# Local and pooled attention ahead of two feed-forward layers: the first stage put into the list schedule, with 1 KB loads by head pair and local products on GpSimd

## The chip, the cores and the metric

The kernel runs on one core of a Trainium2 chip. The metric is the device time in microseconds of one execution; smaller is better. Engines: PE (TensorE; PEld its weight loads), DVE (VectorE), ACT (ScalarE), POOL (GpSimd) and SP (SyncE, which issues most DMAs).

## The reference

Queries, keys and values are float32 arrays of 4 x 8 x 576 x 64 (batch, heads, rows, head size).

```python
q_d = q.reshape(B, H, Sd, factor, D).mean(axis=3)     # factor 4; k_d, v_d likewise
out_d = sm_attn(q_d, k_d, v_d)                        # softmax attention over 144 pooled rows
out_up = np.repeat(out_d, factor, axis=2)
mask = np.abs(pos[:, None] - pos[None, :]) < factor   # local attention: 7 neighbours
scores = np.where(mask, scale * np.matmul(q, k.transpose(0, 1, 3, 2)), -1000000000.0)
out_local = np.matmul(softmax(scores), v)
x = out_up + out_local                                # 2304 tokens x 512
h = x @ w_in;  x = (h - np.tanh(h)) @ w_out           # 512 -> 2048 -> 512
h = x @ w_in2; y = (h * np.cos(h)) @ w_out2           # 512 -> 2048 -> 512
```

## The kernel before

The 2304 tokens are cut into chunks: the first 512 rows of each batch make chunks 0 to 3 (128 partitions by four rows; chunk 1 is worked on as two halves of 256), and the last 64 rows of all four batches (the left-over rows) make chunk 4. Each feed-forward matrix is split into a high and a low float32r part, so each product is three matmuls of 128x128 weights against 512 (or 256) columns.

**The first stage** (`first_attention`, lines 452 to 692) computes the attention of chunk 0 with PE. Per head pair `u` (NP = 4) there are pooled steps: `P.s` (scores, maximum), `P.e` (three exponentials with sums), `P.n` (product on POOL, L398), `P.t` and `P.t2` (transposes), `P.v` (product with the summed values). Per block `i` of 64 rows (NB = 8) there are local steps: `b_s` (mask and scores into a bank of three), `b_m` (maximum, subtraction, exponential in the bank), `b_n` (sum, reciprocal, product into SBUF, all on DVE, L618 to L621), `b_t` (transpose). Per pair of blocks, `b_v` multiplies with v, adds the pooled part (L642) and copies to `xh`; `b_l` subtracts to `xl`. The inputs come by `load_nat` (128 rows of all heads, 256 KB, runs of 256 B, L496), are transposed by `tr` (four transposes) and summed by fours in `red_k` (DVE) and `red_q` (POOL); left-over rows come by `load_lo` and go through `tr_l`. `vsum` sums v by fours on POOL (L303, L304).

The order of these steps is written by hand: each has a time (`keyed`, L656 ff.), the steps are sorted by it and emitted, and each PE step is followed by one matmul `idle<-zero` (`warm`, L479), which computes nothing. Three weight tiles are prepared (`W1.tick`) and chunk 1's first loads issued (`early`, L1118) at times of the same list. In one engine, instructions run in the order in which they were emitted.

**The planner** (`Plan`, L33) orders the rest of attention and the first feed-forward layer. A step has an engine, a duration, a due time `t`, the steps it comes after and the buffers it takes. `run` picks, for each engine, among the steps that could start within `SLACK` of the earliest the one with the smallest due time, and emits the earliest of these. Due times come from constants: `LENGTHS` and `SPANS` for chunks, `LOADEARLY`, `WEARLY` and `WLOAD` for loads and weights. Attention of the later chunks uses POOL for products of 128x896 (`prod_s` L709, `prod_v` L758) and DVE for their sums. The first layer's groups (`group`, L981) write `h` tiles of two buffers; the first two groups run in halves of 256 columns, the four halves in the order a, a, b, b. The weights take ACT (L218, L220, L237), DVE (L228) and POOL (L244) each. The second layer follows, in the order of the program.

## Time and profile before

| what | us |
|---|---|
| median of 3 runs | 902.53 (901.45 to 902.73) |
| the profiled execution | 904.6 |
| its span | 902.7 |
| PE, PEld busy | 886.4, 747.0 |
| DVE, ACT, POOL busy | 571.4, 486.2, 406.2 |

The page gives busy time by engine, the span in 40 slices, the DMA queues, the chain of work that ended last, and the costliest groups of instructions. In the rows below, `x` with a number counts instructions; "[2.24 <-DVE gl L1000]" is idle time ahead of an instruction and what ended it. The granted clock is a share of 2.4 GHz. Matmuls overlap, so the busy time of PE counts time that is shared.

### The profile page before, as it was taken

The page shows a single profiled execution, that of the slowest core. Times are in us where ns is not written, and L with a number is a line of the kernel's source. Part 1 is how long each engine was busy: PE and PEld are TensorE (multiplying, and loading weights), DVE is VectorE, ACT ScalarE, POOL GpSimd, SP SyncE. Part 2 cuts the span into 40 slices and gives each one's busy share as a digit, 9 for nine tenths or more (in the row PEclk, how much of TensorE's full clock was granted, in tenths as well). Part 3 has the DMA queues.
Part 4 walks back from the last instruction along what each step waited for, and adds up shares of the span by engine and source line. Part 5 has one row for each costly group of instructions (what it writes and reads, how often), then busy time and mean ns, then how long its engine had stood idle before and what let it go on. Part 6 is the DMA issues. An engine that isn't in the chain of part 4 may idle for free.

```text
span 902.7 us, 13649 instructions
## 1 busy us (share of the span) xinstructions
PE 886.4 (98%) x4954; PEld 747.0 (83%) x4954; DVE 571.4 (63%) x958; ACT 486.2 (54%) x1024; POOL 406.2 (45%) x447
## 2 busy tenths in 40 slices
PE   9989998999999999999999999999999999999997
PEld 5677785999998888888899888888888888888896
DVE  5789878889999863852245577454536453655453
ACT  4768887335444433373269876454535453544464
POOL 7489999998988971730026343011101110111110
PEclk9999999999999999999999999999999999999999
DMA  9687746423332231461037431010001100100100
GB/s 211 198 281 236 238 132 191 146 86 114 93 104 80 64 85 31 143 186 34 1 120 232 126 108 47 1 47 16 32 1 46 47 1 6 42 23 1 47 2 24
DMA packets 65957, 81.73 MB, mean 91 GB/s; under 512 B 21984, under 2 KB 46566, under 8 KB 65890
## 3 DMA queue, kind: packets, MB, share of 16 engines
q1 hardware_dynamic: 64562, 76.01, 27.8%
q0 software_dynamic: 1232, 4.72, 1.7%
q8 instruction: 39, 0.64, 0.3%
...
## 4 chain that ended last, share of the span: by engine, by line
PE 88%; POOL 4%; ACT 3%; DVE 2%; SPq 1%; DMA 1%; issue 1%; POOLq 0%; ACTq 0%; DVEq 0%
PE h L951 42%; PE oacc L1213 22%; PE acc L977 20%; POOL pr L709 1%; PE pa_s L377 1%; PE pa_t L408 1%; SPq L496 1%; POOL o L244 1%; POOL pr L758 1%; PE pa_x L796 1%; DMA lpt<-in_v_dram 1%; ACT pe L390 1%; PE pa_v L436 1%; PE pa_v L439 0%; DMA raw<-in_moe_w_in_dram 0%
## 5 line engine op out<-in xcount | busy, mean ns | idle before, releaser
L1213 PE MATMUL oacc<-o,i 128*128 128x512 f32 x864 | 209.0, 391 | 0.0
L951 PE MATMUL h<-xh,i 128*128 128x256 f32 (+1 forms) x784 | 203.6, 338 | 2.8 <-DVE gl L1000 2.2
L977 PE MATMUL acc<-gh,o 128*128 128x512 f32 (+1 forms) x768 | 203.2, 342 | 0.9 <-POOL o L244 0.8
L1228 POOL TENSOR_SCALAR y<-y 128x512 f32<-128x512 f32 (+1 forms) x80 | 46.3, 579 | 327.4 <-ACT y L1226 312.2
L951 PE MATMUL h<-x2h,i 128*128 128x512 f32 (+1 forms) x640 | 192.9, 369 | 0.0
L1213 PEld LDWEIGHTS oacc<-o,i 128*128 128x128 f32 x864 | 161.1, 188 | 34.6 <-ACT i L964 0.4
L951 PEld LDWEIGHTS h<-xh,i 128*128 128x128 f32 x784 | 135.8, 191 | 18.5 <-issue 2.9
L977 PEld LDWEIGHTS acc<-gh,o 128*128 128x128 f32 x768 | 134.0, 191 | 17.9 <-POOL o L244 2.9
L951 PEld LDWEIGHTS h<-x2h,i 128*128 128x128 f32 x640 | 116.7, 188 | 21.7
L709 POOL TENSOR_TENSOR pr<-qt,kt 128x896 f32<-128x896 f32 x56 | 119.1, 2137 | 31.0 <-DVE o L762 24.6
L951 PE MATMUL h<-xl,i 128*128 128x256 f32 (+1 forms) x392 | 131.3, 335 | 0.3 <-DVE xl L649 0.3
L977 PE MATMUL acc<-gl,o 128*128 128x512 f32 (+1 forms) x384 | 129.5, 338 | 0.3 <-DVE gl L1000 0.2
L951 PE MATMUL h<-x2l,i 128*128 128x512 f32 (+1 forms) x320 | 117.9, 369 | 0.0
L758 POOL TENSOR_TENSOR pr<-vt,s 128x896 f32<-128x896 f32 x56 | 107.5, 1939 | 1.6 <-DVE o L762 0.3
L1233 DVE TENSOR_TENSOR h<-h,rr 128x512 f32<-128x512 f32 (+1 forms) x80 | 51.6, 645 | 81.8 <-ACT rr L1232 81.6
L1231 ACT ACTIVATE rr<-rr 128x512 f32<-128x512 f32 (+1 forms) x80 | 47.1, 589 | 100.4 <-DVE rr L1230 100.2
L951 PEld LDWEIGHTS h<-xl,i 128*128 128x128 f32 x392 | 74.8, 191 | 7.5 <-DVE xl L649 0.6
L968 ACT ACTIVATE gh<-h 128x512 fp32r<-128x512 f32 x72 | 42.9, 596 | 70.3 <-PE acc L977 62.5
L977 PEld LDWEIGHTS acc<-gl,o 128*128 128x128 f32 x384 | 73.4, 191 | 8.4 <-DVE gl L1000 1.1
L1235 DVE TENSOR_TENSOR i<-h,i 128x512 fp32r<-128x512 f32 (+1 forms) x80 | 50.7, 634 | 45.5 <-ACT i L964 45.4
L994 ACT ACTIVATE th<-h 128x512 f32<-128x512 f32 x64 | 38.2, 597 | 72.5 <-PE h L951 72.4
L1226 ACT ACTIVATE y<-h 128x512 f32<-128x512 f32 (+1 forms) x80 | 44.2, 553 | 59.9 <-PE h L951 59.7
(183 smaller groups left out, 1243.2 us busy)
## 6 DMA issues: line engine op xcount, KB each, us to landing
...
kt<-in_k_dram SPq DMA_DIRECT2D x16, 256.0 KB, 3.7
vt<-in_v_dram SPq DMA_DIRECT2D x16, 256.0 KB, 4.2
...
out_dram<-os SPq DMA_DIRECT2D x16, 256.0 KB, 2.1
```

The source lines that it names most:

```text
L709: nc.gpsimd.tensor_tensor(out=pr.rearrange("p j f d -> p j (f d)"), in0=view(L["q", h], [[0, OFF], [1, 2 * D]], off=f * D), in1=view(L["k" ...
L758: nc.gpsimd.tensor_tensor(out=pr.rearrange("p f d j -> p j f d"), in0=view(L["v", h], [[D, OFF], [D, 2], [1, D]], off=f * D), in1=view(L[" ...
L951: nc.tensor.matmul(hp[:, cs], lhsT=wt[:, kk * 128:(kk + 1) * 128], rhs=xt, start=(kk + c == 0), stop=(kk == KD - 1 and c == 2))
L968: nc.scalar.activation(gh, hp, AF.Copy)
L977: nc.tensor.matmul(acc[e], lhsT=wt[:, e * 128:(e + 1) * 128], rhs=gt, start=(f == 0 and i == 0), stop=(f == KF - 1 and i == 2))
L994: nc.scalar.activation(th, hp, AF.Tanh)
L1213: nc.tensor.matmul(acc[t], lhsT=gt[:, t * 128:(t + 1) * 128], rhs=wt, start=(g == 0 and a_ == 0), stop=(g == KF - 1 and a_ == 2))
L1226: iy = nc.scalar.activation(y, hp, AF.Copy, scale=INV_TWO_PI, bias=ROUND)
L1228: ip = nc.gpsimd.tensor_scalar(out=y, in0=y, scalar1=-ROUND, scalar2=-TWO_PI_HI, op0=ALU.add, op1=ALU.mult)
L1231: nc.scalar.activation(r, r, AF.Abs)
L1233: nc.vector.tensor_tensor(out=hp, in0=hp, in1=r, op=ALU.mult)
L1235: nc.vector.tensor_tensor(out=G[f][1], in0=hp, in1=G[f][0].bitcast(F32), op=ALU.subtract)
```

## The change

- `load_nat` fetches the 512 rows of one head pair, four rows (1 KB) to a partition and head. `tr` makes eight matmuls with the identity of it, 64 output partitions each, and the copies put the rows back in order.
- `red_q` writes its sum straight into `qz`; the factor 1/16 moves into the scores' maximum (a small DVE operation) and the exponential's scale. `pooled_q` on ACT goes; `left_q` becomes a step per head pair.
- `b_m` writes its exponentials to SBUF (`ce`, four buffers); `b_n` sums from there, and POOL makes the product (`NORMB` is all "P").
- `lpt` is zeroed by DVE and not by POOL.
- All steps of the first stage are steps of the one planner, with due times by the longest chain behind them (`tails`). The planner runs until the stage's last `xl` is placed, then the pools are exchanged, and it runs on. The filler matmuls (448 columns) follow the plan's gaps on PE in the first run, and no longer each step.
- The first five weight tiles and chunk 1's loads and products are steps too, open to the planner from the start. The first layer's due times begin at `TB` = 44. Buffers and constants of the later stages stay.

The diff, cut to its core:

```diff
+    def tails(self, steps, end):
+
+        tail = {}
+        for o in reversed(steps):
+            d = o.size / 350e3 + 2.1 if o.size else o.dur
+            o.tail = max(d + LATENCY, o.tail_min) + tail.get(o, 0.0)
+            o.t = end - o.tail
+            for a in o.after:
+                tail[a] = max(tail.get(a, 0.0), o.tail)
+            if o.prev is not None:
+                tail[o.prev] = max(tail.get(o.prev, 0.0), o.tail - o.prev.dur)
...
+            if fill and o.eng == "PE":
+                fill(int((r - self.free["PE"] - 0.1) / 0.2))
...
+            if self.ps_t:
+                nc.vector.tensor_scalar(out=m, in0=m, scalar1=1.0 / (R * R), scalar2=None, op0=ALU.mult)
...
-                nc.scalar.activation(e_[:, i, :], a[:, i, :], AF.Exp, bias=m[:, i:i + 1], accum_out=rs[:, i:i + 1])
+                nc.scalar.activation(e_[:, i, :], a[:, i, :], AF.Exp, bias=m[:, i:i + 1], scale=1.0 / (R * R) if self.ps_t else 1.0, accum_out=rs[:, i:i + 1])
...
-                nc.tensor.matmul(idle, lhsT=zero[:, 0:128], rhs=zero)
+                nc.tensor.matmul(idle[:, 0:448], lhsT=zero[:, 0:128], rhs=zero[:, 0:448])
...
-        def load_nat(nm, t):
-            G[nm, t] = g = lp.tile([128, H, D], F32, tag="g", name=nm + "g", bufs=12)
-            nc.sync.dma_start(out=g, in_=rows_of(q if nm == "q" else k, 0, 128 * t, 128))
+        def load_nat(nm, u):
+            G[nm, u] = g = lp.tile([128, 2, R, D], F32, tag="g", name=nm + "g", bufs=12)
+            nc.sync.dma_start(out=g.rearrange("p e f d -> p e (f d)"),
+                              in_=(q if nm == "q" else k)[0, 2 * u:2 * u + 2, 0:512, :].rearrange("h (p f) d -> p h (f d)", f=R))
...
+            G["vl"] = xp.tile([128, H, R, D], F32, tag="xl", name="lpt")
+            nc.vector.memset(G["vl"], 0.0)
...
-        def tr(nm, t):
-            g = pairs(G.pop((nm, t)))
-            a = ps_a.tile([128, NP, 128], F32, tag="a", name="pa_tr")
-            for u in range(NP):
-                nc.tensor.transpose(a[:, u, :], g[u], ident)
+        def tr(nm, u):
+            g = G.pop((nm, u))
+            a = ps_a.tile([128, R, 128], F32, tag="a", name="pa_tr")
+            for f in range(R):
+                for e in range(2):
+                    nc.tensor.matmul(a[64 * e:64 * e + 64, f, :], lhsT=g[:, e, f, :], rhs=ident)
+            yield
             if nm == "q":
-                nc.scalar.activation(qT[:, :, 128 * t:128 * t + 128], a, AF.Copy, scale=0.125)
+                nc.scalar.activation(qT[:, u, :].rearrange("p (g f) -> p f g", f=R), a, AF.Copy, scale=0.125)
+            elif KEVAC[u] == "A":
+                nc.scalar.activation(kT[:, u, R - 1:R - 1 + 512].rearrange("p (g f) -> p f g", f=R), a, AF.Copy)
             else:
-                nc.vector.tensor_copy(kT[:, :, R - 1 + 128 * t:R - 1 + 128 * t + 128], a)
+                nc.vector.tensor_copy(kT[:, u, R - 1:R - 1 + 512].rearrange("p (g f) -> p f g", f=R), a)
...
+        def red_q(u):
+            half = lp.tile([128, 128, 2], F32, tag="qh", name="qh", bufs=2)
+            q4 = qT[:, u, :].rearrange("p (g f) -> p g f", f=R)
+            nc.gpsimd.tensor_tensor(out=half, in0=q4[:, :, 0:2], in1=q4[:, :, 2:4], op=ALU.add)
+            for e in range(2):
+                p0 = 64 * e
+                nc.gpsimd.tensor_tensor(out=qz[p0:p0 + 64, u, QW * e:QW * e + 128], in0=half[p0:p0 + 64, :, 0], in1=half[p0:p0 + 64, :, 1], op=ALU.add)
+
+        def left_q(u):
+            for e in range(2):
+                nc.gpsimd.tensor_scalar(out=view(qz, [[2, LG], [1, 2]], off=u * 3 * 128 + QW * e + 128, p0=64 * e, n=64),
+                                        in0=view(klq, [[1, LG], [0, 2]], off=NP * 64 + u * 64, p0=64 * e, n=64),
+                                        scalar1=float(R * R), scalar2=None, op0=ALU.mult)
...
-        def pooled_q():
-            for e in range(2):
-                nc.scalar.activation(qz[64 * e:64 * e + 64, :, QW * e:QW * e + 128], qd[64 * e:64 * e + 64], AF.Copy, scale=1.0 / (R * R))
-            for u in range(NP):
-                P.left_q(u)
...
-            exps.append(nc.scalar.activation(s, s, AF.Exp).ins)
+            yield
+            G["e", i] = lp.tile([128, NP, NK], F32, tag="ce", name="ce", bufs=4)
+            nc.scalar.activation(G["e", i], s, AF.Exp)
...
+            rs = sums[:, i]
...
-            nc.vector.tensor_tensor(out=et, in0=s, in1=view(r, [[1, NP], [0, NK]]), op=ALU.mult)
+            yield
+            eng = nc.gpsimd if NORMB[i] == "P" else nc.vector
+            eng.tensor_tensor(out=et, in0=et, in1=view(r, [[1, NP], [0, NK]]), op=ALU.mult)
...
-        with_pe = (tr, tr_l, b_s, b_t, b_v)
-        keyed = [(-9.08, masks), (-2.95, load_vl), (-1.21, load_vg), (13.94, pooled_k), (14.57, pooled_q), (23.6, load_w)]
...
+        add, run = plan.add, plan.chain
+        n0 = len(plan.steps)
+        marks = []
+        small, large = 1.9, 1.1
+        ld, xt, xl, red, vs, up_, sc, bt = {}, {}, {}, {}, {}, {}, {}, {}
+        for t in range(NT_):
+            for nm in "kq":
+                ld[nm, t] = add("SP", 0.47, 0.0, lambda nm=nm, t=t: load_nat(nm, t), new=[("g", f"{nm}g{t}")], size=128 * 2048 * large)
+        for j in range(2):
+            for nm in "kq":
+                ld[nm, "l", j] = add("SP", 0.94, 0.0, lambda nm=nm, j=j: load_lo(nm, j), new=[("k" if j else "g", f"{nm}l{j}")], size=128 * 2048 * small)
+        ld["vg"] = add("SP", 0.47, 0.0, load_vg, size=128 * 8192 * large)
+        ld["vl"] = add("SP", 1.9, 0.0, load_vl, size=64 * 8192 * large)
+        for i in range(NB):
+            ld["vw", i] = add("SP", 0.47 if i else 1.41, 0.0, lambda i=i: load_vw(i), new=[("g", f"vw{i}")], size=NK * 2048 * small)
+        for t in range(NT_):
+            for nm in "kq":
+                a = f"tr{nm}{t}"
+                xt[nm, t] = run(tr(nm, t), 0.0, [
+                    ("PE", 0.92, dict(new=[("ps_a", a)], use=[f"{nm}g{t}"])), ("DVE", 0.72, dict(use=[a])) if nm == "k" and KEVAC[t] == "D" else ("ACT", 0.63, dict(use=[a]))],
+                    after=[ld[nm, t]])[-1]
+                marks += [(o, EARLY[t]) for o in (ld[nm, t], xt[nm, t].prev, xt[nm, t])]
+        late = []
+        for j in range(2):
+            for nm in "kq":
+                a = f"trl{nm}{j}"
+                k0 = len(plan.steps)
+                xl[nm, j] = run(tr_l(nm, j), 0.0, [
+                    ("PE", 0.87, dict(new=[("ps_a", a)], use=[f"{nm}l{j}"])), ("DVE", 0.32 if j else 0.5, dict(use=[a])) if nm == "k" else ("ACT", 0.3, dict(use=[a]))],
+                    after=[ld[nm, "l", j]])[-1]
+                late += [ld[nm, "l", j]] * j + plan.steps[k0:] * j
+        for t in range(NT_):
+            red["k", t] = add("DVE", 0.64, 0.0, lambda t=t: red_k(t), after=[xt["k", t]])
+            red["q", t] = add("POOL", 1.45, 0.0, lambda t=t: red_q(t), after=[xt["q", t]], new=[("qh", f"qh{t}")])
+            red["l", t] = add("POOL", 0.45, 0.0, lambda t=t: left_q(t), after=[xl["q", 0]])
+            marks += [(red[x, t], EARLY[t]) for x in "kql"]
+        pk = add("POOL", 0.24, 0.0, pooled_k, after=[xl["k", 0]])
+
+        for nm, o_ in (("vg", vd), ("vl", vl)):
+            for u in range(NP):
+                vs[nm, u] = add("POOL", 1.2, 0.0, lambda o_=o_, nm=nm, u=u: vsum(o_, nm, u), after=[ld[nm]])
...
+        for i in range(NB):
+            c = f"cs{i}"
+            k0 = len(plan.steps)
+            o = add("PE", 0.9, 0.0, lambda i=i: b_s(i), new=[("ps_1", c)],
+                    after=list(xt.values()) + [xl["k", 0]] * (i == NB - 1))
+            o = run(b_m(i), 0.0, [("DVE", 0.92, dict(use=[c], new=[("cm", f"cm{i}")])), ("ACT", 0.4, dict(use=[c], new=[("ce", f"ce{i}")]))], after=[o])
+            o = run(b_n(i), 0.0, [("DVE", 0.88, dict(use=[f"ce{i}"], new=[("cr", f"cr{i}")])),
+                                  ("POOL", 0.8, dict(use=[f"cr{i}"])) if NORMB[i] == "P" else ("DVE", 0.46, dict(use=[f"cr{i}"]))], after=o)[-1]
+            bt[i] = run(b_t(i), 0.0, [("PE", 0.47, dict(new=[("ps_a", f"cpt{i}")], use=[f"ce{i}"])), ("ACT", 0.62, dict(use=[f"cpt{i}"]))], after=[o])[-1]
+            marks += [(x, BLOCK[i]) for x in plan.steps[k0:]]
+        out = []
+        for j in range(NB // 2):
+            a = f"po{j}"
+            o = run(b_v(j), 0.0, [
+                ("PE", 1.1, dict(new=[("ps_1", a)], use=[f"vw{i}" for i in (2 * j, 2 * j + 1)], after=[bt[2 * j], bt[2 * j + 1], ld["vw", 2 * j], ld["vw", 2 * j + 1]])),
+                ("PE", 0.95, dict(use=[a], after=list(up_.values()))) if UADD[j] == "P" else ("DVE", 0.72, dict(use=[a], after=list(up_.values()))), ("ACT", 0.62, dict(use=[a], new=[("x", "x0")] if j == 0 else [], after=list(vs.values())))],
+                prev=o[0] if j else None)
+            o.append(add("DVE", 0.7, 0.0, lambda j=j: b_l(j), after=o[-1:], use=[a]))
+            out.append(o[-1])
+            o[0].tail_min = 1.2
+        plan.tails(plan.steps[n0:], FEND)
+        marks += [(o, VSUM) for o in vs.values()] + [(o, LOADFIRST) for o in plan.steps[n0:] if o.eng == "SP"] + [(o, OUTS) for o in out]
+        for o, d in marks:
+            o.t += d
+        for o in late:
+            o.t = LATEL - o.tail
+        return out, warm
...
-    TL = 26.5
-    HALVES, XLAST, RAWLAST = 2, 1.68, 3.91
+    TB, FEND, LATEL = 44.0, 20.0, 60.0
+    NORMB = "PPPPPPPP"
+    KEVAC = "DDDD"
+    UADD = "DDDD"
+    LOADFIRST, VSUM, OUTS = 0.00, 0.00, 0.00
+    EARLY = 0.00, 0.50, 1.00, 1.50
+    POOLED = -3.00, -2.50, -2.00, -1.50
+    BLOCK = 0.00, 0.20, 0.40, 0.60, 0.80, 1.00, 1.20, 1.40
+    NF, WFIRST, WLOADF = 5, 3.0, 16.0
+    HALVES = 2
...
+                o = plan.add("PE", mm, t, lambda j=j: second(j), after=[done[j]] + [gate] * (ci == 0) + [wready.get(("o", f)) for f in fs],
...
+            if k < NF:
+                t, slot = need(kind, f) - WFIRST, "raw"
+            ld[k] = plan.add("SP", 0.4, t - (WLOAD if k >= NF else WLOADF), lambda: W1.load(raw_a), after=[gate] if k == NF else [], prev=ld.get(k - 1), new=[(slot, names[k])], size=128 * 4096)
+            bg[k] = plan.chain(W1.begin_parts(), t - 9.0, [
+                ("ACT", 0.65, dict(new=[("wf", wf)] + [("ps_a", wp)] * (k >= NF), use=[names[k]], after=[ld[k]])), ("ACT", 0.67, dict(use=[names[k]]))])
+            md[k] = plan.chain(W1.mid_parts(), t - 7.0, [
+                ("DVE", 0.7, dict(use=[names[k], wf] + [wp] * (k >= NF))),
+                ("POOL" if k < 3 else "ACT", 0.63, dict(use=[wf], new=own))], after=bg[k])
...
-    add_events(first_attention(chunks[0]), 0.0)
-    loaded = {}
-
-    def early(h, which):
-        loaded[h, which] = load_qkv(chunks1[1], h, which, True)
-
-    events += [(TL + 0.02 * i, 0, lambda h=h, x=x: early(h, x)) for i, (h, x) in enumerate([(h, x) for h in range(3) for x in "qk"] + [(h, "v") for h in range(2)])]
-    events += [(TE + TD * i, 0, lambda: W1.tick(raw_a, nc.gpsimd)) for i in range(KE)]
-    events.sort(key=lambda x: x[0])
     sched = tc.manual_schedule()
     sched.__enter__()
-    run_events(1e9)
+    plan = Plan(dict(q=3, k=3, v=3, pr=2, s=3, m=2, r=2, o=8, qkd=2, vd=3, kT=1, pe=1, pt=1, pm=2, pr_=2, up=7, ps_a=2, ps_h=2, acc=4,
+                     th=2, gh=2, gl=2, x=1, raw=2, wf=3, i15=1, o15=1, i14=1, o14=1,
+                     g=12, qh=2, ps_1=3, cm=3, cr=3, ce=4), {}, dict(PE=5.0, ACT=6.4, DVE=2.5, POOL=7.3, SP=0.0))
+    first, warm_ = first_attention(plan, chunks[0])
+    gate = Step(None, 0.0, 0.0, None, (), None, (), 0)
...
+    plan.run(AHEAD, first, warm_)
+    gate.start = gate.end = max(o.start for o in first)
...
```

## Rows read from the trace of the kernel before

**Rows 1.** Stage windows: length; busy by engine (instructions); granted clock; DMA share; GB/s

```profile
5.00:25.00 20.00, 19.37 (x183) 14.15 (x182) 14.30 (x35) 8.95 (x24) 14.36 (x32) 1.00 1.07 225
30.00:35.00 5.00, 4.59 (x55) 2.76 (x57) 3.96 (x15) 3.38 (x13) 3.31 (x6) 1.00 1.07 368
...
7.77:50.87 43.10, 41.15 (x480) 30.25 (x479) 32.55 (x83) 26.44 (x75) 24.75 (x44) 1.00 0.79 201
...
57.30:62.00 4.70, 4.69 (x14) 3.71 (x15) 4.26 (x6) 2.63 (x8) 4.70 (x5) 0.64 0.97 316
130.00:162.00 32.00, 28.07 (x132) 20.63 (x131) 25.99 (x51) 23.68 (x63) 30.91 (x33) 0.95 0.58 177
162.00:503.00 341.00, 340.66 (x2148) 304.59 (x2147) 229.64 (x361) 161.13 (x371) 210.41 (x181) 1.00 0.34 103
```

(In the windows the engines stand in the order PE, PEld, DVE, ACT, POOL.)

**Rows 2.** Timeline at the first layer's start: start, length, engine, line, instruction, idle

```profile
48.14 0.20 PEld L951 LDWEIGHTS h<-xh,i 128*128 128x128 f32 x1
...
57.31 0.47 PE L951 MATMUL h<-xh,i 128*128 128x512 f32 x1 [2.24 <-DVE gl L1000]
```

**Rows 3.** Groups by line, DVE, 0 to 51: busy us, mean ns | idle before

```profile
L618 DVE TENSOR_REDUCE cs<-cs 128x4 f32<-128x280 f32 x8 | 3.6, 454 | 1.7 <-ACT cs L611 1.7
L621 DVE TENSOR_TENSOR ce<-cs,cr 128x280 f32<-128x280 f32 x8 | 3.6, 449 | 0.3
...
L649 DVE TENSOR_TENSOR xl<-pa_o,xh 128x512 fp32r<-128x512 f32 x4 | 2.7, 687 | 0.8 <-ACT xh L645 0.7
...
L392 DVE TENSOR_SCALAR pa_s<-pa_s 128x3 f32<-128x3 f32 x4 | 0.7, 166 | 2.0 <-ACT pe L390 1.9
```

**Rows 4.** Groups by line, POOL, 0 to 51.4

```profile
L244 POOL TENSOR_TENSOR i<-wf,i 128x512 fp32r<-128x512 f32 x3 | 3.9, 1300 | 0.0
L303 POOL TENSOR_TENSOR vg<-vg 128x256 f32<-128x256 f32 x4 | 2.9, 728 | 0.0
...
L582 POOL TENSOR_TENSOR qh<-qT 128x256 f32<-128x256 f32 x4 | 2.5, 613 | 3.4 <-ACT qT L558 3.3
L235 POOL CAST i<-wf 128x512 fp32r<-128x512 f32 x3 | 1.8, 613 | 9.9 <-DVE wf L228 9.9
L304 POOL TENSOR_TENSOR vl<-lpt 128x128 f32<-128x128 f32 x4 | 1.8, 456 | 0.3
...
L295 POOL MEMSET lpt<- 128x2048 f32 x1 | 1.8, 1814 | 0.0
L369 POOL COPY qz<-klq 64x32 f32<-64x32 f32 x8 | 1.7, 206 | 0.4
L583 POOL TENSOR_TENSOR qd<-qh 128x128 f32<-128x128 f32 x4 | 1.6, 400 | 0.3
...
L398 POOL TENSOR_TENSOR pe<-pe,pr__434 128x432 f32<-128x432 f32 x1 | 0.9, 907 | 0.0
```

**Rows 5.** Groups by line, PE, 0 to 48.14

```profile
L482 PE MATMUL idle<-zero 128*128 128x512 bf16 x41 | 16.6, 450 | 1.3 <-DVE zero L527 1.3
```

**Rows 6.** Timeline of PE, a transposed load and the first two local blocks

```profile
9.68 0.63 PE L556 MATMUL pa_tr<-ident,kg 128*128 128x128 f32 x4 [0.29 <-DMA kg<-in_k_dram]
...
10.36 0.28 PE L598 MATMUL cs<-mask_b,ident_b 128*128 128x280 bf16 x1
...
14.62 0.28 PE L598 MATMUL cs<-mask_b,ident_b 128*128 128x280 bf16 x1
```

**Rows 7.** Timeline of POOL, the first product for chunk 1

```profile
51.45 2.60 POOL L709 TENSOR_TENSOR pr<-qt,kt 128x896 f32<-128x896 f32 x1
```

**Rows 8.** Groups by line, POOL, 57 to 160

```profile
L709 POOL TENSOR_TENSOR pr<-qt,kt 128x896 f32<-128x896 f32 x15 | 31.8, 2129 | 0.0
```

**Rows 9.** Waits of PE, 130 to 162: us in total, times, longest

```profile
PE pa_v L436 <- ACT pe L425: 1.3, 2, 0.7
...
PE acc L977 <- POOL o L244: 0.6, 2, 0.3
```

**Rows 10.** DMA issues, 0 to 25: count, KB each, median us to landing

```profile
kg<-in_k_dram SPq DMA_DIRECT2D x4, 256.0 KB, 3.0
```

250 lines of the change are left out of this document (104 added, 146 removed).

## The prediction

> **What bounds the kernel now.** I read the page's slices and chain first: TensorE (PE) is busy in nearly all forty slices, and the feed-forward lines make up most of the chain. So only the stretches where PE does something else, or waits, or runs at the lower clock can pay. The stage windows put them in order [rows 1]. From 162.00 to 503.00 PE is busy 340.66 of 341.00 us: nothing that this change moves is felt there. Ahead of it stand three places.
>
> First, the stage before the first feed-forward matmul, whose weights load at 48.14 [rows 2]. PE looks full in it, but 41 of its matmuls, 16.6 us, are `idle<-zero` and compute nothing [rows 5]. No engine is full: between the first and the last instruction of VectorE's (DVE's) chain, 7.77 to 50.87, DVE is busy 32.55 of 43.10 us, 76%, ScalarE (ACT) 26.44 and GpSimd (POOL) 24.75 [rows 1]. This stage is bound by chains that wait for each other in an order written by hand.
>
> Second, right after the start, PE stands 2.24 us for `gl` [rows 2], and then runs near the lower of its two levels, 1.2 GHz: the grant is 0.64 on the mean of 57.30 to 62.00 [rows 1]. Third, the end of the first chunk: in 130.00 to 162.00 PE is busy 28.07 of 32.00 at a mean grant of 0.95, beside POOL at 30.91 [rows 1]. PE's waits there name the pooled chain on ACT, and POOL only with 0.6 us [rows 9].
>
> The profiled execution took 904.6 us, span 902.7, so 1.9 lie outside the span; the median of the runs is 902.53, 2.1 below it. Sums are made against 904.6 and then lowered by 2.1.
>
> **The change part by part.**
>
> *Loads.* Eight loads of 256 KB of queries and keys go from 256 B runs to 1 KB runs. With the short runs the DMA engines are full (share 1.07) at 225 GB/s in 5 to 25 us; with the long runs of the next chunk's loads they are as full at 368 GB/s in 30 to 35 [rows 1]. 2.1 MB take 9.3 us at the first rate and 5.7 at the second: 3.6 us of DMA time. Not all of it is on the path. Each local block now needs all eight transposes, since a load holds a head pair and no longer a stretch of rows; before, the first block began on PE at 10.36 and the second at 14.62 [rows 6]. By 368 GB/s the eight loads have landed 3.0 (median landing of `kg` [rows 10]) + 5.7 = 8.7 us after the first issue, which stands at the start of the program, and the last transpose and copy end at about 11.5: later than the first block was, earlier than the second. I count 1 us for the stage, bounds 0 and 3.6. The left-over rows stay in short runs. The loads of `v`, of weights and of the next chunk's q and k stay the same in number, but SyncE issues them as soon as it is free and a slot is, in order of due time: the next chunk's land earlier and come behind all that the first stage needs early.
>
> *DVE.* Eight products `ce` of 0.449 go (-3.6); four 128x3 operations come, 0.166 each by the row of that shape (+0.7); the sums now read SBUF, 0.454 from PSUM before, taken unchanged [rows 3]. The zeroing of `lpt` moves to DVE, some 1.8 us if it goes as on POOL [rows 4], and DVE's chain begins at 7.77, so the wait for the first keys hides it; without that cover it costs its length. Net -2.9: 32.55 becomes 29.65.
>
> *POOL.* It gets the eight products. No row has this shape on POOL; 128x256 takes 0.613 and 128x432 takes 0.907, which bound it; between them in proportion 0.65, eight times 5.2 us, bounds 4.9 and 7.3. The memset of 1.81 goes; `red_q` writes its second sum in two halves of at most 0.400 each, 4 x 0.4 = +1.6; the left-over queries stay at eight of 0.206. Sum +5.0. What POOL must do before the last local product: sums of q 4 x (0.613 + 0.8) = 5.65, left-over 1.65, sums of v 8 x (0.727 + 0.456) = 9.46, pooled products 4 x 0.907 = 3.63, local products 5.2, and for the weights three casts of 0.613 and two subtractions of 1.300, 4.4: 30.0 us [rows 4].
>
> A row of 512 columns takes 1.300 on POOL [rows 4] beside 0.687 for such a subtraction on DVE [rows 3]. The Trainium skill, GPSIMD Engine Reference, section Performance versus the Vector engine, speaks against this step: an operation on two tensors takes 1.96 times as long there as on the Vector engine. By that rule eight products cost an estimated 8 x 0.449 x 1.96 = 7.0 us in place of 5.2, and the forecast would lie some 2 us higher; the trace agrees at 512 columns (1.89) and puts less on the smaller shapes.
>
> *PE and ACT.* Four transposes of a load take 0.63 [rows 6]; they become eight half-width matmuls, 0.63 if the halves run beside each other, 1.26 if not; I take 0.9, so 8 x 0.27 = +2.2 us. The fillers that followed each step go, and come back only where the plan sees PE idle. ACT loses two copies of `qz`. The exponentials leave PSUM, so a block's bank is free after them and no longer after the product. Neither engine sets the end: without fillers PE has 41.15 - 16.6 + 2.2 = 27 us shown (more where a filler lay over another matmul), ACT 26.
>
> *The order.* The list planner places the first stage too, with due times from the longest chain behind each step. I keep DVE's 76% as what chains of this kind reach: 29.65 / 0.755 = 39.3 us, from 6.5 (1 us earlier, by the loads) to 45.8 in place of 50.87. The first feed-forward matmul comes 2.7 before that end (50.87 - 48.14), so at 43.1. POOL gives another bound: from about 7.6, when the first queries are there, 30.0 us without a gap, then transposes, copy, product with v, add and split, of which 2.2 lie before the first matmul: 39.8; with 15% of gaps 45.1. I take 45.0, near the later one, since POOL gets the work: **-3.1**, bounds -5.0 and the rival on the slow side.
>
> *After the start.* The 2.24 us wait and the slow matmuls stay: `h` still has two buffers, and the halves of the first two groups still run a, a, b, b; no fillers are left by then. At 130 to 162 PE loses 3.9 us idle and 32 x 0.05 = 1.6 by the clock, 5.5 in all [rows 1]. POOL's products for the next chunk, 2.13 each [rows 8], began at 51.45 [rows 7]; now one or two can run in the first stage's gaps, and POOL's lag shrinks by that. Since PE's waits there mostly name ACT [rows 9], I take **-1.0**, bounds 0 and -5.5.
>
> Sum: 904.6 - 3.1 - 1.0 = 900.5 profiled, **898.4** as a median.
>
> **The rivals.**
>
> *More comes back (0.17).* The stage reaches DVE's bound (-5.0), and POOL's lead takes most of the loss at 130 to 162 (-4.5): 902.5 - 9.5 = 893.0. POOL's 30.91 of 32.00 there speaks for it; against it, that POOL's own name stands on so little of PE's waiting.
>
> *Given back (0.15).* The stage shortens by 3.1, but the second chunk waits for POOL, whose work has no gap to shorten; PE then idles 3.1 more at 130 to 160: 902.5. Against it speaks that POOL's products start earlier by as much.
>
> *POOL crowded, slower (0.14).* The planner takes whichever step can start first, so a product of 2.13 us goes ahead of a local product that is ready a moment later. POOL works in order: queued behind are the local products, and for them wait the transposes and products with v of the last blocks. With four such products the start is at 45.1 + 4 x 2.13 = 53.6, 5.5 late; what was done early gives back perhaps 2.5 at 130 to 160: 905.5. It decides from about one such product on: (48.14 - 45.1) / 2.13 = 1.4. One more thing can lengthen it: a product beside `wf` on DVE took 2.60 in place of 2.13 [rows 7, 8].
>
> *Clock (0.08).* Fillers stand only in gaps that the plan foresees. If the real gaps differ, PE falls to 1.2 GHz within the stage; a stretch like 57.30 to 62.00 costs 4.7 x 0.36 = 1.7 us [rows 1]. With three of them the gain of 3.1 becomes a loss of 2: 904.5.
>
> **How the numbers follow.** The forecast has 0.46. The 0.2% that a measurement can tell from no change is 1.8 us. Faster gets 0.63: the forecast's cases but for 0.04, the first rival, 0.04 of the second. Within 0.2%: 0.17, mostly the second rival. Slower: 0.20, nearly all of the last two. The range 892.5 to 905.0 cuts more than half of the slow cases and the best end of the first rival, some 0.2 in all.
>
> **What would show it.** The first `h` matmul between 43 and 46.5; `ce` products on POOL at 0.6 to 0.75; DVE over 80% busy from 7 us to the last `xl`; the q and k loads moving over 300 GB/s before 10 us; still 2 us of wait on `gl` and a grant near 0.64 behind it. I am wrong on the order if four or more `pr` products stand on POOL ahead of the last local product and the first `h` comes after 48; wrong on what follows if PE's idle time in the 32 us around the end of the first chunk differs from 3.9 by more than 3.

## The result and the profile after

The changed kernel takes 909.64 us (median of 4 runs, 906.92 to 910.12) against 902.40 (901.45 to 902.73) before: 1.0076 times as long, 95% interval 1.0054 to 1.0098. Forecast were 898.4 us and a range of 892.5 to 905.0; it is slower, and outside the range. The profiled execution, the shortest of the four, took 906.92 us, span 905.2.

The stage windows of the changed kernel (length; busy time of PE, PEld, DVE, ACT, POOL with counts; granted clock; DMA share; GB/s) answer to [rows 1]:

```profile
7.77:52.00 44.23, 39.50 (x499) 29.49 (x496) 34.60 (x80) 24.74 (x71) 36.63 (x58) 0.92 0.87 204
...
16.00:22.00 6.00, 5.82 (x73) 4.60 (x72) 5.78 (x15) 2.79 (x13) 5.42 (x11) 1.00 1.21 120
...
25.00:30.00 5.00, 3.17 (x37) 2.18 (x37) 3.78 (x15) 2.60 (x10) 4.76 (x8) 1.00 1.12 265
30.00:35.00 5.00, 3.88 (x52) 2.58 (x52) 3.58 (x11) 3.09 (x9) 4.92 (x7) 1.00 1.11 283
35.00:40.00 5.00, 5.00 (x32) 2.65 (x31) 3.69 (x5) 2.37 (x9) 3.68 (x5) 0.59 0.86 270
40.00:45.00 5.00, 5.00 (x70) 3.84 (x70) 3.53 (x12) 3.15 (x8) 2.80 (x4) 0.73 0.30 114
...
100.00:130.00 30.00, 26.98 (x126) 21.10 (x126) 23.21 (x36) 26.31 (x56) 28.73 (x26) 1.00 0.59 184
130.00:162.00 32.00, 30.04 (x153) 23.78 (x151) 25.89 (x50) 24.77 (x62) 30.44 (x31) 1.00 0.57 179
162.00:503.00 341.00, 339.13 (x2134) 303.09 (x2135) 229.21 (x359) 159.49 (x368) 207.00 (x178) 1.00 0.33 101
```

POOL is now full where it was a third idle (4.76 and 4.92 of 5 us in 25 to 35; 3.33 and 3.31 before). PE waits there, and right behind that wait the grant falls to 0.59 on the mean of 35 to 40: PE "busy 5.00 of 5.00" there is no more work (32 matmuls), but work at little more than half speed. The timeline of PE shows the waits (start, length, instruction, idle time before it and what ended it):

```profile
5.10 1.97 PE L581 MATMUL pa_tr<-ident,qg 128*64 128x128 f32 x32
7.47 1.09 PE L581 MATMUL pa_tr<-ident,kg 128*64 128x128 f32 x16 [0.41 <-ACT qT L584]
...
15.17 1.74 PE L400 MATMUL pa_s<-kd,qz 128*128 128x144 f32 x12
16.83 1.09 PE L581 MATMUL pa_tr<-ident,kg 128*64 128x128 f32 x16
17.86 0.93 PE L506 MATMUL idle<-zero 128*128 128x448 bf16 x4
18.63 0.28 PE L627 MATMUL cs<-mask_b,ident_b 128*128 128x280 bf16 x1
...
29.27 0.55 PE L433 MATMUL pa_t<-ident,pe 128*128 128x128 f32 x3 [1.82 <-POOL pe L423]
...
34.34 0.55 PE L433 MATMUL pa_t<-ident,pe 128*128 128x128 f32 x3 [1.12 <-ACT pe L450]
...
51.30 1.15 PE L672 MATMUL pa_o<-cp,vw 70*64 70x64 f32 x32
52.39 0.39 PE L1029 MATMUL h<-xh,i 128*128 128x256 f32 x1
...
61.53 0.47 PE L1029 MATMUL h<-xh,i 128*128 128x512 f32 x1 [2.39 <-DVE gl L1078]
```

Behind the first of these waits stands POOL's queue: the pooled product that PE waits for had its reciprocal from DVE at 26.45, and POOL, in the order of the plan, first made two sums of `v`:

```profile
26.27 0.18 DVE L418 RECIPROCAL pr__459<-pa_s 128x3 f32<-128x3 f32 x1
...
28.31 0.91 POOL L423 TENSOR_TENSOR pe<-pe,pr__459 128x432 f32<-128x432 f32 x1
...
45.78 0.65 POOL L653 TENSOR_TENSOR ce<-ce,cr 128x280 f32<-128x280 f32 x1 [0.39 <-DVE cr L650]
...
50.57 1.87 DVE L689 TENSOR_TENSOR xl<-pa_o,xh 128x512 fp32r<-128x512 f32 x3
```

The first local block starts at 18.63 (10.36 before [rows 6]). The weights of the first feed-forward matmul load at 52.38 (48.14 [rows 2]): 4.2 late, where 3.1 early was forecast. What follows got shorter: 905.2 - 52.38 = 852.8 us against 902.7 - 48.14 = 854.6.

Two numbers of every run help below: its span times its mean granted clock, and what that leaves of the span, an upper bound of what the lower clock took (it counts a slow stretch as lost even where PE only waited in it). For the kernel before the medians are 897.9 and 2.7 us (81 runs beside the experiments, 902.84 us median), for the changed one 900.5 and 6.4. So the change pays twice: at least some 2.6 us of waiting, and up to 3.7 of clock.

### The profile page after: what moved, and what is told of

Read it like the earlier page. It is cut to its first block, busy times and chain, and to the rows that moved or that the text cites. A ratio compares the mean times of both kernels' runs of the same rounds, so it can differ in the third digit from the quotient of the medians.

```text
span 905.2 us, 13834 instructions
## 1 busy us (share of the span) xinstructions
PE 883.9 (98%) x5036; PEld 748.4 (83%) x5036; DVE 574.0 (63%) x955; ACT 485.1 (54%) x1022; POOL 412.4 (46%) x458
## 4 chain that ended last, share of the span: by engine, by line
PE 90%; POOL 3%; DVE 3%; DMA 1%; issue 1%; SPq 1%; ACT 0%; DVEq 0%; POOLq 0%; ACTq 0%
PE h L1029 43%; PE oacc L1281 22%; PE acc L1055 20%; PE pa_s L400 1%; POOL pr L794 1%; POOL pr L843 1%; PE pa_t L433 1%; DMA raw<-in_moe_w_in_dram 1%; PE pa_v L461 1%; PE pa_x L881 1%; DMA qg<-in_q_dram 1%; PE pa_v L464 1%; POOL i L276 0%; PE pa_tr L581 0%; POOL o L276 0%
```

## The experiments

"First h" is the first feed-forward matmul in the profiled execution; the ratio is to the kernel before on the same chip. The profiled execution is one run. In e1, e2, e3, e6, e10, e11, e12, e13 and e15 it was the longest, in e4 and in the changed kernel the shortest, so a first h and a window stand for that run and not for the median.

| run | first h | median us | ratio, 95% interval | span x clock | rest |
|---|---|---|---|---|---|
| kernel before | 48.2 | 902.84 | 1 | 897.9 | 2.7 |
| changed kernel | 52.4 | 909.64 | 1.0076 (1.0054 to 1.0098) | 900.5 | 6.4 |
| e1 later loads | 52.9 | 906.86 | 1.0061 (1.0034 to 1.0088) | 902.1 | 2.7 |
| e2 fillers, 25 to 40 | 54.5 | 911.86 | 1.0102 (1.0076 to 1.0128) | 905.0 | 5.0 |
| e3 products on DVE | 50.6 | 914.52 | 1.0122 (1.0100 to 1.0143) | 904.5 | 7.3 |
| e4 no early chunk 1 | 48.0 | 912.94 | 1.0114 (1.0081 to 1.0148) | 903.0 | 8.2 |
| e5 old order, products on POOL | 65.3 | 921.08 | 1.0175 (1.0149 to 1.0201) | 900.1 | 19.3 |
| e6 old order, new loads | 52.5 | 908.82 | 1.0052 (1.0038 to 1.0066) | 903.5 | 2.7 |
| e7 list, old loads | 54.5 | 920.32 | 1.0176 (1.0159 to 1.0194) | 907.2 | 10.6 |
| e8 DMA at 230 | 47.8 | 914.85 | 1.0119 (1.0103 to 1.0134) | 910.3 | 2.3 |
| e9 no products | 49.0 | 906.50 | 1.0041 (1.0026 to 1.0057) | 899.8 | 4.5 |
| e10 one vw load | 55.7 | 913.56 | 1.0122 (1.0089 to 1.0155) | 900.7 | 10.0 |
| e11 no fillers | 54.9 | 912.81 | 1.0088 (1.0056 to 1.0120) | 897.7 | 14.6 |
| e12 fillers in waits | 52.7 | 910.11 | 1.0078 (1.0055 to 1.0102) | 902.3 | 6.4 |
| e13 other order | 52.8 | 902.59 | 0.9992 (0.9977 to 1.0007) | 897.6 | 2.7 |
| e14 other order | 51.4 | 905.89 | 1.0039 (1.0021 to 1.0057) | 902.6 | 1.8 |
| e15 old order, no fillers | 56.4 | 904.77 | 1.0030 (1.0010 to 1.0050) | 896.4 | 6.3 |
| e16 e12, sums in SBUF | 53.7 | 911.32 | 1.0096 (1.0079 to 1.0113) | 903.2 | 6.4 |
| e17 e13, sums in SBUF | 47.0 | 902.87 | 0.9999 (0.9986 to 1.0012) | 896.6 | 4.5 |
| e18 e17, fillers | 48.2 | 901.86 | 0.9998 (0.9984 to 1.0012) | 897.8 | 2.7 |

**What makes the stage late: loads, clock, products, early work of chunk 1 (e1 to e4).**

```diff
# e1: chunk 1's q, k and v loads not before 28 us of the plan
-            plan.last[which] = plan.add("SP", 0.4, t, ...
+            plan.last[which] = plan.add("SP", 0.4, t, ..., after=[held]
# e2: at least one filler ahead of each PE step planned in 25 to 40
-                fill(int((r - self.free["PE"] - 0.1) / 0.2))
+                fill(max(int((r - self.free["PE"] - 0.1) / 0.2), 1 if 25.0 < r < 40.0 else 0))
# e3
-    NORMB = "PPPPPPPP"
+    NORMB = "DDDDDDDD"
# e4: chunk 1's products with k wait for the first stage
-after=lds, prev=p_, ...
+after=lds + [gate], prev=p_, ...
```

> The loads of the next chunk's q, k and v may not be issued before 28 us of the plan; nothing else is edited. DMA theory (the next chunk's loads crowd the first stage's and the weights' loads; ScalarE's first weight step then stands in order in front of the pooled steps): the first two raw tiles land by 27 us where they land at 30.4 and 33.3 now, ScalarE's waits for them (0.2 and 1.6 us) go, the first h matmul comes at 49.5 to 50.5 where it stands at 52.46, time 2 to 3 us below the changed kernel. GpSimd theory (the products moved to it set the stage): the first h stays at 52 to 53, time unchanged. Clock theory: the gain is there only if the grant of 35 to 42 us rises from 0.6 to 1.

> At least one filler matmul ahead of each PE step that the plan starts between 25 and 40 us; before, only in planned gaps. Clock theory (PE idles in gaps that the plan didn't foresee, falls to 1.2 GHz from 35 to 42 us, and its pooled and local steps set the end there): the grant of 35 to 42 stays above 0.95, the first h comes 1.5 to 2.5 us earlier than 52.46. DMA and GpSimd theories: the waits stay, fillers of 0.2 us stand in front of real work, the first h comes no earlier (52.5 to 53.5).

> The eight local products go back to VectorE; exponentials stay in SBUF, order by the planner. GpSimd theory (GpSimd is full from 15 to 35 us and the product's transposes wait for it): the first h comes 1.5 us or more ahead of 52.46 and the time falls by as much. DMA and clock theories: no earlier than 52, and up to 1 us later, since VectorE gets 3.6 us of work.

> The next chunk's first products on GpSimd may not be placed before the first stage's end (they run at 32.5 and 46.4 now). If GpSimd is crowded by them: the weight step wf at 46.7 on VectorE takes 0.7 us and not 2.3, the first h comes 1 to 2 us earlier, and the end of the first chunk loses up to 3 us of it. DMA theory: the first h moves by 1 us at most, the time by less than 1 us.

e1 removes ACT's two waits for `raw` (0.17 and 1.60 us in 30 to 34). Its median lies 2.8 us lower, but by the ratios the gain is 1.4 and the intervals overlap, so it is not shown to be faster; its profiled run, with a grant of 0.50 to 0.61 in 30 to 45, starts no earlier. e2 keeps the grant at 1.00 in 35 to 60, and is later. e3 starts 1.8 us earlier, e4 4.4, e4 with a grant of 1.00 from 20 to 55; both end higher. In e4 what had been moved out of the stage is missing behind it: PE is busy 20.85 of 25 us in 50 to 75, against 22.51 in the changed kernel. The last point is the first sign that the start does not set the time.

**The parts alone (e5 to e7).** e5 and e6 put one part each into the kernel before, e7 takes the loads out of the changed one.

```diff
# e5, in the kernel before
-            exps.append(nc.scalar.activation(s, s, AF.Exp).ins)
+            G["e", i] = lp.tile([128, NP, NK], F32, tag="ce", name="ce", bufs=4)
+            exps.append(nc.scalar.activation(G["e", i], s, AF.Exp).ins)
...
-            nc.vector.tensor_tensor(out=et, in0=s, in1=view(r, ...), op=ALU.mult)
+            nc.gpsimd.tensor_tensor(out=et, in0=et, in1=view(r, ...), op=ALU.mult)
# e6, in the kernel before
-        def load_nat(nm, t):
+        def load_nat(nm, u):
...
-                (tr, "q", (-9.07, 12.44, 4.09, 7.14)),
+                (tr, "q", (-8.56, -7.56, -6.56, -5.56)),
# e7, in the changed kernel
-        def load_nat(nm, u):
+        def load_nat(nm, t):
...
-                    after=list(xt.values()) + [xl["k", 0]] * (i == NB - 1))
+                    after=[xt[nm, t] for nm in "kq" for t in sorted({max(0, (64 * i - 3) // 128), i // 2, min(3, (64 * i + 66) // 128)})] + [xl["k", 0]] * (i == NB - 1))
```

In e6 `load_nat`, `tr`, `red_k` and `red_q` are those of the changed kernel (the sum of q still goes to `qd`), and all eight loads and transposes stand ahead of the first block. In e7 they are those of the kernel before, and each block waits for its row blocks only.

> One part alone on the kernel before: the order stays written by hand and the loads stay row blocks; the local exponentials go to SBUF and the eight products to GpSimd. Theory (the order of the list schedule loses the time, the parts are small): DVE loses 8 x 0.449 = 3.6 us, POOL gains 8 x 0.65 = 5.2 us in a stage in which it has 18 us free; the first h matmul between 47.5 and 49.5 us (48.14 before), total within 1.5 us of the kernel before. Rival (the product on GpSimd costs the time): products wait behind sums of v and queries on POOL, h at 51 or later, total 4 us or more above.

> One part alone on the kernel before: q and k of chunk 0 loaded by head pair in 1 KB runs, eight half-width transposes per load, strided copies; all eight transposes stand ahead of the first local block in the order by hand, otherwise the order stays, the products stay on DVE. Theory (the order loses the time): loads finish about 3 us earlier, copies on DVE cost 4 x 0.39 = 1.6 us more, the first block starts a few us later; h between 46.5 and 50, total within 2 us of the kernel before. Rival (the loads by head pair cost it, since every block needs all eight transposes): h at 51 or later, total 4 us or more above.

> The changed kernel with one part undone: row-block loads in 256 B runs, four full transposes per load and sums per row block, each local block needing only its row blocks; list schedule and products on GpSimd as in the changed kernel. Theory (the order loses the time): first h still at 50.5 or later, total 906 to 912. Rival (the loads by head pair cost it): first h at 48 or earlier, total 903 or less.

Both parts cost time in the old order, as the rivals of e5 and e6 put it in numbers; undoing the loads in the new order costs 10.7 us more (9.0 by the ratios), more than the theory had and against the rival of e7. So no part has a price of its own, it depends on the order around it. POOL's timeline in e5 shows how eight instructions of 0.65 us can cost 17:

```profile
33.14 0.65 POOL L621 TENSOR_TENSOR ce<-ce,cr 128x280 f32<-128x280 f32 x1 [3.35 <-ACT pe L390]
37.46 0.65 POOL L621 TENSOR_TENSOR ce<-ce,cr 128x280 f32<-128x280 f32 x1 [3.67 <-DVE cr L620]
```

POOL has little to do (7.09 of 15 us busy in 35 to 50), but each product stands in its queue at a place made for the shorter old chain; POOL waits there for ACT and DVE, and the sums of v and pooled products behind it wait too (the rival had it the other way round, products waiting behind sums). The grant is 0.68 in 35 to 50 and 0.50 in 50 to 65, and by the table nearly all of the loss (19.3 - 2.7 = 16.6 us) can be the lower clock behind these waits.

e6 shows the transposes by head pair without anything between them but a filler each:

```profile
5.20 1.10 PE L558 MATMUL pa_tr<-ident,kg 128*64 128x128 f32 x16
...
14.62 1.09 PE L558 MATMUL pa_tr<-ident,qg 128*64 128x128 f32 x16
15.65 0.39 PE L482 MATMUL idle<-zero 128*128 128x512 bf16 x1
15.88 0.28 PE L599 MATMUL cs<-mask_b,ident_b 128*128 128x280 bf16 x1
...
52.48 0.47 PE L952 MATMUL h<-xh,i 128*128 128x256 f32 x1
```

Eight times 1.09 and a filler fill 5.20 to 15.88: the first block is 5.5 us later than in [rows 6], the first h 4.3, the total 5.3.

**The planner's DMA rate (e8).**

```diff
-            d = o.size / 350e3 + 2.1 if o.size else o.dur
+            d = o.size / 230e3 + 2.1 if o.size else o.dur
...
-                self.dma = o.end = max(self.dma, r + 1.2) + o.size / 350e3
+                self.dma = o.end = max(self.dma, r + 1.2) + o.size / 230e3
```

> The changed kernel whose planner reckons DMA at 230 KB/us in place of 350; nothing else. Theory (the plan puts steps of the next chunk and of the weights where their data has not come, and what is queued behind them waits): the waits of ACT for raw (0.17 + 1.60 us) and of PE behind them (1.12) go, first h between 48.5 and 51, total 904 to 908. Rival (the loads or the products cost it): first h within 1 us of 52.4, total within 2 us of 909.6.

h starts at 47.84, earlier than in the kernel before, at a grant of 1.00, and the median is 5 us above the changed kernel's. From 48 to 175 us PE waits behind the start, for POOL's parts of the weights above all (`i L276`; in the changed kernel 0.3 us). The wait's row (us in total, times, longest) and the windows:

```profile
PE h L1029 <- POOL i L276: 3.9, 4, 1.6
...
50.00:75.00 25.00, 21.14 (x107) 17.37 (x106) 23.27 (x40) 18.41 (x42) 22.31 (x26) 0.93 0.79 247
75.00:100.00 25.00, 23.85 (x122) 19.12 (x120) 21.04 (x37) 19.59 (x46) 21.42 (x22) 1.00 0.82 266
100.00:130.00 30.00, 26.64 (x125) 20.15 (x123) 22.43 (x39) 25.96 (x58) 29.47 (x30) 1.00 0.60 185
```

**One kind of load or instruction left out, the order kept (e9 to e11).** e9 leaves out the eight products on POOL, e10 seven of the eight loads of the windows of v, e11 all fillers after the first ten.

```diff
# e9
-            eng.tensor_tensor(out=et, in0=et, in1=view(r, [[1, NP], [0, NK]]), op=ALU.mult)
+            if i < 0:
+                eng.tensor_tensor(out=et, in0=et, in1=view(r, [[1, NP], [0, NK]]), op=ALU.mult)
# e10
         def load_vw(i):
+            if "vw" in G:
+                G["vw", i] = G["vw"]
+                return
# e11
-            if fill and o.eng == "PE":
+            if fill and o.eng == "PE" and r < 0:
```

> The changed kernel with the eight local products on GpSimd left out, everything else in the same order on every engine (the output is not normalized there). Theory (GpSimd's work up to the end of chunk 1 sets the time, since POOL is over 90% busy from 20 to 165 us): 8 x 0.65 = 5.2 us less on POOL, the end of chunk 1 (first copy of its results, 211.0 in the changed kernel, 208.5 before) 3 to 5 us earlier, total 904 to 907. Rival (waits on transfers and the clock set it): first h less than 1 us earlier, total within 1.5 us of 909.6.

> The changed kernel with seven of the eight loads of the windows of v left out (the first loaded tile serves all blocks, so the output differs), everything else in the same order. About 1 MB in 256 B runs goes, 7 to 9 us of full DMA at the 107 to 135 GB/s of the stretch 16 to 22 us. Theory (full DMA queues make the stage late): loads of the weights land some 5 us earlier, ACT's waits for raw (0.17 and 1.60 us) go, first h at 50.5 or earlier (52.4), total 2 us or more below 909.6. Rival (engines, not transfers, set the stage): first h within 1 us of 52.4 and total within 1.5 us.

> The changed kernel with the fillers after the first ten left out, everything else in the same order. Theory (the clock costs the stage about 2 us): the granted clock in 10 to 50 us falls below the 0.93 mean of the changed kernel, first h 1 to 3 us later than 52.4, total up by as much. Rival (the fillers stand in front of steps that wait for PE and cost more than the clock): first h 1 us or more earlier, total down by 1 to 2 us.

e9 prices all eight products in this order: 3.1 us, with the first h 3.4 us earlier and the end of chunk 1 (first copy of its results) at 209.2 instead of 211.0; the intervals of the two kernels just meet. e10 frees the queues and gets slower; its windows tell why:

```profile
25.00:30.00 5.00, 2.51 (x30) 1.74 (x28) 3.55 (x14) 2.22 (x7) 4.76 (x9) 0.94 0.81 292
30.00:35.00 5.00, 5.00 (x44) 3.41 (x44) 2.12 (x5) 2.53 (x5) 4.92 (x6) 0.50 0.02 4
35.00:40.00 5.00, 5.00 (x28) 2.61 (x26) 4.42 (x11) 2.17 (x7) 3.38 (x5) 0.50 0.18 48
40.00:45.00 5.00, 5.00 (x38) 3.10 (x35) 1.21 (x4) 2.42 (x8) 1.29 (x3) 0.50 0.72 244
```

In 30 to 35 there is hardly a transfer to wait for (4 GB/s); PE waits 2.49 us for POOL's `pe` up to 29.90, the grant is 0.50 for the next 15 us, and the first h comes at 55.7. e11 has the same stretch at 0.50, as the clock theory said; its ratio can't be told from that of the changed kernel. So the lower clock makes this order late. Whether it is also what makes it slow is another question.

**The clock against the order (e12 to e15).**

```diff
# e12: fillers inside the two waits of the timeline above
+                fill(8 if 26.5 < r < 26.6 else 5 if 30.5 < r < 30.6 else int((r - self.free["PE"] - 0.1) / 0.2))
# e13
-                    ("PE", 0.92, dict(new=[("ps_a", a)], use=[f"{nm}g{t}"])), ("DVE", 0.72, dict(use=[a])) ...
+                    ("PE", 1.05, dict(new=[("ps_a", a)], use=[f"{nm}g{t}"])), ("DVE", 1.08, dict(use=[a])) ...
...
-    TB, FEND, LATEL = 44.0, 20.0, 60.0
+    TB, FEND, LATEL = 42.6, 27.1, 50.8
...
-    POOLED = -3.00, -2.50, -2.00, -1.50
+    POOLED = (-7.37, -2.27, -2.13, -1.5)
...
-    LENGTHS = 100.00, 52.17, 50.12, 90.53, 87.05
+    LENGTHS = (104.84, 57.91, 46.81, 90.53, 87.05)
# e15, in the kernel before
-                if fn in with_pe:
-                    warm(1)
```

e13 also sets the left-over queries' duration to 0.65, and changes `EARLY`, `BLOCK`, `LOADFIRST`, `VSUM`, `OUTS`, `WFIRST`, `WLOADF`, the `REDLATE` line, `WEARLY`, `URGENT` and `SPANS`; no step is changed. e14 has another such set, and one of the eight local products on DVE.

> The changed kernel, same order, with eight fillers ahead of the transposes that waited 1.82 us at 29.27 for GpSimd and five ahead of those that waited 1.12 us at 34.34 for ACT; about 0.19 us each, so they lie inside these waits. Theory (the clock makes the stage late): the grant stays at 0.95 or above in 30 to 50 us (0.59 and 0.73 in 35 to 45 of the changed kernel), first h at 49.5 to 51 (52.4), median 904 to 907, and the runs lie closer together. Rival (the order itself): grant up, but first h not before 51.5 and median within 1.5 us of 909.6.

> Every part of the change kept; the planner's durations of the head-pair transposes, copies and left-over queries set to what the trace shows (1.05, 1.08, 0.65 us) and its due-time constants changed with them, so that only the order differs. Theory (the order, as made from too short durations, is what can still be better): first h at 49 to 52, median 903 to 908, at best level with the kernel before. Rival (the parts cost the time in any order): median within 2 us of 909.6 or above.

> As the run before it, with another set of constants and one of the eight local products on DVE. Same expectations: 903 to 908 if the order matters, within 2 us of 909.6 or above if the parts cost it in any order.

> The kernel before with the filler after each PE step of the first stage left out (the first ten stay); order and parts as before. Theory (the clock): PE waits more often, the grant falls below 0.8 somewhere in 20 to 48 us, the first h at 50 to 56 instead of 48.14, total 3 to 8 us above the kernel before. Rival (the clock is no cause): first h up to 2 us earlier, total level or faster.

In e12 the grant stays at 1.00 up to 50 us, and the median at 910. The windows of its profiled run show the lower clock behind PE's next gap, at the start of the first layer:

```profile
35.00:40.00 5.00, 4.90 (x46) 2.79 (x45) 3.78 (x8) 2.81 (x11) 3.30 (x4) 1.00 0.24 68
40.00:45.00 5.00, 4.88 (x97) 3.86 (x93) 4.28 (x15) 4.38 (x10) 3.82 (x6) 1.00 0.70 230
45.00:50.00 5.00, 3.31 (x46) 2.33 (x47) 5.00 (x7) 2.69 (x6) 4.00 (x4) 1.00 0.07 13
50.00:55.00 5.00, 5.00 (x47) 4.33 (x46) 4.06 (x8) 3.86 (x7) 2.79 (x3) 0.59 0.85 282
55.00:60.00 5.00, 5.00 (x33) 5.00 (x33) 2.85 (x4) 1.43 (x6) 4.59 (x7) 0.73 0.78 242
```

The clock isn't all of it: two of e12's runs had a mean grant of 0.997, the value that the kernel before has most often, and still took 907.7 and 908.2 us.

e13 has every part of the change, and only other constants: 902.59 us, 7.0 less than the changed kernel, level with the kernel before. So the parts do not force the loss: another order of the same parts is without it. How much of the 7 us is clock can be read from runs with the same mean grant. At 0.995 the changed kernel took 906.9 and e13 902.8 to 904.4; at 0.991 they took 910.1 and 907.2. By these few runs I estimate about 3 us for the order at an equal clock; the rest goes with the higher grant that e13 has in most runs. The start does not show it: in its profiled run, the longest with 907.2 us, the grant falls to 0.50 and the first h is no earlier (52.8). What the same run does show is less waiting in 100 to 165 us, where PE idles 6.57 us in the changed kernel (3.02 and 3.55, for the weights' parts on ACT and POOL and for chunk 1's `xl` on DVE), 3.93 before, and 2.45 in e13:

```profile
30.00:35.00 5.00, 5.00 (x44) 3.96 (x45) 3.10 (x9) 1.97 (x6) 3.09 (x6) 0.50 0.99 258
...
100.00:130.00 30.00, 30.00 (x151) 24.30 (x150) 22.85 (x39) 24.39 (x58) 27.94 (x27) 1.00 0.54 168
130.00:165.00 35.00, 32.55 (x162) 24.55 (x160) 22.31 (x44) 26.69 (x69) 25.11 (x28) 1.00 0.46 142
```

The row of the changed kernel for the last stretch has POOL at 33.44 of 35 us where e13 has 25.11:

```profile
130.00:165.00 35.00, 31.45 (x165) 25.23 (x164) 28.64 (x54) 25.93 (x66) 33.44 (x33) 1.00 0.60 193
```

e14 ended between the two, at 905.89. e15 is the counter-test: the old order without its fillers loses 1.8 us in the median, less than expected; in its profiled run, the longest with 912.0 us, the grant is 0.74 in 20 to 48 and the start 8.3 us late.

**A wait that the change itself made (e16 to e18).** In e2 and e12 fillers wait, though they compute nothing. Two lines of e2's PE:

```profile
27.78 0.35 PE L506 MATMUL idle<-zero 128*128 128x448 bf16 x1 [0.68 <-DVE cr L650]
...
36.17 0.35 PE L506 MATMUL idle<-zero 128*128 128x448 bf16 x1 [1.12 <-DVE cr L650]
```

The changed kernel keeps the sums of the local blocks (`rs`) in the last columns of the fillers' PSUM tile, so a filler waits for DVE's last use of it, with all of PE behind it.

```diff
-        sums = idle[:, 448:448 + NB * NP].rearrange("p (i u) -> p i u", i=NB)
+        sums = lp.tile([128, NB, NP], F32, name="sums")
# e16 = e12 with it, e17 = e13 with it, e18 = e17 and
+                fill(8 if 26.8 < r < 26.95 else 3 if 22.85 < r < 22.95 else int(...))
```

> e12 with the local sums in SBUF, so that fillers and DVE no longer wait for each other (1.1 us of PE, 1.2 us of DVE in e12). Theory (the order sets the time): first h 1 to 2 us earlier than 52.7, median 906 to 910. Rival (the fillers' waits and the clock together were the cause): first h at 50 or earlier, median 905 or less.

> e13 with the local sums in SBUF. Theory: the fillers' wait of 1.66 us for DVE at 42.8 and DVE's of 2.1 for fillers go; first h 1 to 2 us earlier than 52.8, median 900.5 to 902.5. Rival (off the path, as the first h has not followed the total so far): within 0.7 us of 902.6.

> e17 with eight fillers ahead of the local block that PE waited 2 us for at 27.6 us, and three at about 23 us. Theory (clock): the grant of 0.50 in 30 to 35 and 0.79 to 0.92 up to 50 us goes to 0.95 or above, first h 1 to 3 us earlier than e17, median 899.5 to 901.5, faster than the kernel before by 1.5 to 3 us. Rival (the half clock only moves to the next gap, as in e12): within 0.7 us of e17.

In the order of the changed kernel it brings nothing (911.32). In e13's the profiled run starts at 47.0, and the median stays (902.87); that run had a grant of 1.00 in 20 to 55, where e13's had the low stretch, so the earlier start can't be put down to the sums. For the same reason e18's fillers had no low stretch to remove there. e18 has the lowest median of all, 901.86, but it cannot be told from e17 nor from the kernel before (0.9984 to 1.0012). None of the 18 beats it.

## Why the prediction was wrong

**Loads.** "The last transpose and copy end at about 11.5" is the first step that failed: the first block runs at 18.63. The head-pair transposes take 1.09, not 0.9; the copies that put rows back in order, a term that the sum had at nothing, take 1.08 us on DVE and 1.09 on ACT in place of 0.69 and 0.60; the left-over rows, which I had left out of the sum, are loaded and transposed among them (two of 1.05 to 1.08 on PE, 240 GB/s in 4 to 10 us and not 368); and the plan puts a pooled score of 1.74 ahead of the last transpose. That the next chunk's loads "come behind all that the first stage needs early" failed too: queues full from 4 to 35 us, ACT's weight steps waiting for `raw` (though e1, without these waits, has no clear gain). By arithmetic this is nearly the whole miss at the start, 7.1 of 7.3 us: from first block to first h I had 45.0 - 11.5 = 33.5, and it took 33.8. But e17 starts its first block at 21.18 and h at 47.01, 25.8 later. So the arithmetic is no explanation; "76%" and "15% of gaps" were properties of one order, and I took them as the engines'. (The sum on DVE has a slip, too: 7.77 less 1 is 6.8 and not 6.5.)

**DVE and POOL.** The forecast took the start from POOL's bound: the last local product done at 42.9, the first h 2.2 later. The last product ended at 46.43 in the rows above, and the first h came 6.0 later. In that stretch the last product with v (51.30) waits for DVE's first `xl` (50.57), which frees a bank of PSUM, and `xl` stands on DVE behind a weight's `wf` that took 2.31 us beside a product for chunk 1 (shown in the last section). In e4, without that product, `wf` takes 0.68 us, and the stretch is 1.6 us shorter. The 2.2 was in no row; of the two terms it has the larger error. The products cost 5.6 us on POOL (mean 0.710; 5.2 forecast, bounds 4.9 to 7.3), and the second sums of q 8 x 0.396 = 3.2 as forecast. The left-over queries became a multiplication and cost 2.3 instead of 1.65. DVE did not come down to 29.65: it is busy 34.60 us in 7.77 to 52.00, 78%, since the copies take 4 x 1.08 = 4.3 (4 x 0.69 = 2.8 before), the four 128x3 operations 0.330 each (0.166 forecast), and early work of chunk 1 and the weights lies there. By the rule that the forecast weighed (the Trainium skill, GPSIMD Engine Reference, Performance versus the Vector engine: 1.96 times) the products would be an estimated 7.0; the trace has 5.6 us and, against DVE before, 5.6 / 3.6 = 1.56 [rows 3].

**The start, -3.1.** It came out at +4.2. The larger error is the step behind it, that what the start gains the total gains. Four profiled runs start at 47.0 to 48.2, like the kernel before (e4, e8, e17, e18); they took 910.3, 914.7, 901.2 and 900.5 us. My reading is that what PE waits for up to 165 us, POOL and DVE work for chunk 1 and the weights, has to be done by then in any order; taken out of the stage, it is missing behind it (e4, e8), and a longer gap can bring a stretch of lower clock.

**After the start, -1.0.** Right in sign, 1.7 us less, but not by the forecast's parts alone. In 130 to 162 idle time went from 3.93 to 1.96 and the grant from 0.95 to 1.00; 3.0 us of new idle time stand in 100 to 130. The `gl` wait stayed (2.39), but the slow matmuls behind it, which were to stay, did not: the grant is 1.00 in 58 to 66. At the forecast's price for that stretch this is 1.7 us that it had not counted, so the sign is in part luck.

**From profile to median, -2.1.** The profiled run was the shortest, the median lies 2.7 above it. I carried the offset of a kernel whose mean clock hardly varies (0.995 to 0.998 in most runs) over to one that runs at 0.991 to 0.995. The 11.2 us missed are: start 7.3, after the start -0.7, outside the span -0.2, offset 4.8.

**The rivals.** "Clock" (0.08) named the mechanism that the profile shows, fillers in planned gaps while the real ones lie elsewhere, with a price too low for the median (904.5); e12 shows that it isn't enough. "Given back" (0.15) is what e4 and e8 did; that e13 ended at its 902.5 is a coincidence, since e13's profiled start was not early. "POOL crowded" (0.14) was to decide from about one product of chunk 1 ahead of the last local one: there was one, at 32.49, and the start without it came 4.4 us earlier (e4). So it was right on the start; its 2.5 for what early work gives back is too low, since e4 ends 3.3 later in the median. The sign set for a wrong order, four such products, did not come although the start was late: it was tied to one cause. What stays open: which of e13's constants matter, and whether its gain in 100 to 165 us comes from the first stage or from the later chunks' due times, which differ too. The constants of the kernel before were not varied, so level does not mean that the parts are worth nothing, nor that they cost nothing.
